# Attention's loads in another order: values and their shifted copy ahead of later K and Q

## Chip, core and metric

One core of a Trainium2 chip runs the whole program. Its engines are TensorE (PE, matrix products; PEld is its weight load), VectorE (DVE), ScalarE (ACT), GpSimd (POOL) and SyncE (SP). SP computes nothing here: it issues nearly all DMAs of the kernel, and 16 DMA engines carry them out. The metric is the device time of one execution in microseconds; lower is better.

## What is computed

The reference, cut to what matters. A windowed attention with 32 global tokens (4 batches, 8 heads, 512 local positions, head dimension 64) is followed by two feed-forward nets over 2176 tokens:

```python
def _attn_ref(q_l, k_l, v_l, q_g, k_g, v_g):
    k_all = np.concatenate([k_g, k_l], axis=2)
    v_all = np.concatenate([v_g, v_l], axis=2)
    out_g = np.matmul(sm(scale * np.matmul(q_g, k_all.transpose(0, 1, 3, 2))), v_all)
    s_ll = np.where(np.abs(pos[:, None] - pos[None, :]) <= 32, scale * q_l @ k_l^T, -1e9)
    s_lg = scale * np.matmul(q_l, k_g.transpose(0, 1, 3, 2))
    a_l = sm(np.concatenate([s_lg, s_ll], axis=-1))
    return np.concatenate([out_g, np.matmul(a_l, v_all)], axis=2)
...
x = attention output, 2176 x 512
h = x @ moe_w_in;   x = (h * cos(h)) @ moe_w_out
h = relu(x @ moe2_w_in);   result = (h * h) @ moe2_w_out
```

The weights come as 64-bit values, which the kernel reads as pairs of 32-bit words (`raw`) and converts.

## The kernel before, in words

The work on the attention is cut into 40 items (lines 667 to 677): for each group of four heads (8 groups, two for each batch) four local items, two for each pair of heads, and one global item. A pair of heads is p, a group is g = p // 2, so a group takes five items. One loop (line 1365) walks over steps s, some 3 us each. In a step every stage works on another item: `CFG['order']` (line 27) is the order of the stages inside a step, and `CFG['lag']` (line 29) says by how many steps a stage runs behind an item's scores. So TRK (transposing K on PE, tile tk) runs three steps ahead of the scores S (line 393), TRQ (transposing Q, tile tq) two steps ahead, SM (softmax) with them, TM (transposing the probabilities, tile tw) two steps behind, TE (ACT's copy of them to SBUF, tile tws) three, OM (the products with the values, tile o, or og for a global item) four. The order of the instructions of every engine is thus written out by hand; only what one engine needs of another is waited for.

Four of the stages are loads: LK, LQ and LV load K, Q and V of the group g + 2 (`load_k` line 252, `load_q` line 261, `load_v` line 267), and CV (`copy_v`, line 278) copies V inside SBUF, shifted by 64 rows: tile va to tile vb. All four are DMAs that SP issues, in the order of the program. A K takes five DMAs (one of 32 KB, one of 96 KB, three of 128 KB), a Q four of 128 KB, a V six, the copy two of 256 KB, the global values (`load_vg`, tile vgz, line 284) four of 32 KB, the global Q (`load_qgn`, line 384) and the tails of K (`load_ktn`, line 381) one of 64 KB each. K and Q have two buffers each, kn and qn, and V has two, va and vb.

K and Q of the groups 0 and 1, V of group 0 and its copy are issued ahead of the loop (lines 618 to 639). V of group 1 and its copy are issued inside the loop, by two lines at the end of a step (1423 to 1426).

SP issues one more kind of load in the loop: stage BG loads a first weight block (`conv_load`, line 110, tile raw, 512 KB) at step 5, a second at step 8, and four more. They are placed by a small planner, `piece` (line 1304): at step 5 + 3 * i at the earliest, with the conversion of a block three steps behind its load or later. That conversion is ACT's `conv_s` (line 147, tile cc) and POOL's `conv_u` (line 142, tile wf), also of stage BG, then DVE's `conv_v` and `conv_o` (lines 151 and 156) and POOL's `conv_c` (line 163). Inside a step ACT does TE, then BG, then KEV (copying K's transposes), then SM.

In the banks of PSUM tk, tq and tw take turns (`BT`, two banks), so a tw may start when ACT or DVE has copied out what stood in its bank two turns before; scores have three banks (`BS`).

Of the kernel before, what the change touches and what calls it, by code (L numbers as in the profile page):

```python
# [23 lines left out]
TWOPI = 2.0 * math.pi  # L24


CFG = {'order': ['CV', 'LQ', 'S', 'TE', 'BG', 'LK', 'OM', 'TRK', 'KEV', 'CC', 'SM',
           'RC', 'NM', 'CB', 'LV', 'OE', 'TRQ', 'QE', 'KC', 'TM'],
 'lag': {'S': 0,
         'TRK': -3,  # L30
         'TRQ': -2,
# [7 lines left out]
         'TE': 3,  # L39
         'OM': 4,  # L40
         'OE': 4,
         'LK': 0,
         'LQ': 1,
         'LV': 8,
         'CV': 11},
 'ndv': 1,
# [6 lines left out]
def kernel(  # L53
# [166 lines left out]
    BT, BG, BS, BO = (0, 1), (2,), (3, 4, 5), (6, 7)  # L220
# [20 lines left out]
    def whole(dst, src, c0, queues):  # L241

        n = dst.shape[2]
        if n == 2:
            for h, queue in enumerate(queues):
                queue.dma_start(dst[:, c0:4, h], src[h].rearrange("(c p) d -> p c d", p=P))
        else:
            for c in range(c0, 4):
                r = P * (c - c0)
                queues[0].dma_start(dst[:, c], src[:, r : r + P].rearrange("h p d -> p h d"))  # L250

    def load_k(gi, h=0, n=4, queues=(nc.sync, nc.sync)):
        b, g = gi // 2, slice(4 * (gi % 2) + h, 4 * (gi % 2) + h + n)
        if gi not in kn:
            kn[gi] = fp.tile([P, 4, 4, D], F32, tag="kn", name="kn", bufs=2)
        t = kn[gi][:, :, h : h + n]
        nc.sync.dma_start(t[0:SG, 0], k_g[b, g].rearrange("h p d -> p h d"))
        nc.sync.dma_start(t[SG:P, 0], k_l[b, g, 0 : P - SG].rearrange("h p d -> p h d"))
        whole(t, k_l[b, g, P - SG : SL - SG], 1, queues)

    def load_q(gi, h=0, n=4, queues=(nc.sync, nc.sync)):
        b, g = gi // 2, slice(4 * (gi % 2) + h, 4 * (gi % 2) + h + n)
        if gi not in qn:
            qn[gi] = fp.tile([P, 4, 4, D], F32, tag="qn", name="qn", bufs=2)
        whole(qn[gi][:, :, h : h + n], q_l[b, g], 0, queues)

    def load_v(gi):
        b, h0 = gi // 2, 4 * (gi % 2)
        va, g = VA[gi % 2], slice(h0, h0 + 4)
        nc.sync.dma_start(va[0:SG, 0], v_g[b, g].rearrange("h p d -> p h d"))  # L270
        for c in range(5):
            r0, r1 = (SG if c == 0 else 0), (SG if c == 4 else P)
            nc.sync.dma_start(
                va[r0:r1, c],
                v_l[b, g, P * c - SG + r0 : P * c - SG + r1].rearrange("h p d -> p h d"),
            )
# [14 lines left out]
    def tr_k(p):  # L291
        b, kk = divmod(p, NPAIR)
        tk = bank(BT, "tk")
        for c in range(4):
            nc.tensor.transpose(  # L295
                tk[:, c * P : (c + 1) * P],
                kn[p // 2][:, c, 2 * (p % 2) : 2 * (p % 2) + 2].rearrange("p h d -> p (h d)"),
                ident,
            )
        t = ep.tile([P, 8, KTB], F32, tag="kT", name="kT", bufs=3)  # L300
        kT[p] = t
        tks[p] = tk
# [3 lines left out]
    def k_evac(p):  # L306
# [4 lines left out]
        if p == 0:  # L311
# [6 lines left out]
            )  # L318
        if CFG["kb"] == "A":
            nc.scalar.activation(  # L320
                t[:, :, 128:KTB], tk[:, 0:SG].unsqueeze(1).to_broadcast([P, 8, SG]), AF.Copy
            )
        elif CFG["kb"] == "D":
            nc.vector.tensor_copy(
# [3 lines left out]
    def k_copy(p):  # L328
        if p == 0:
            return  # L330
        t = kT[p]
        one = dict(scalar1=1.0, scalar2=1.0, op0=ALU.mult, op1=ALU.mult)
        nc.gpsimd.tensor_scalar(t[:, 0:7, 64:128], t[:, 1:8, 0:64], **one)
        if CFG["kb"] == "P":
            nc.gpsimd.tensor_scalar(
                t[:, :, 128:KTB], t[:, 0, 0:SG].unsqueeze(1).to_broadcast([P, 8, SG]), **one
            )
        if p > 1:
            k_tail(p)
# [7 lines left out]
    def tr_q(p):  # L347
        tq = bank(BT, "tq")
        for c in range(4):
            nc.tensor.transpose(  # L350
                tq[:, c * P : (c + 1) * P],
                qn[p // 2][:, c, 2 * (p % 2) : 2 * (p % 2) + 2].rearrange("p h d -> p (h d)"),
                ident,
            )
        qT[p] = ep.tile([P, SL], F32, tag="qT", name="qT", bufs=3)
        return [lambda: nc.vector.tensor_copy(qT[p], tq)]
# [12 lines left out]
    def prep_ktail(b):  # L369
        nc.scalar.activation(ktail[:, :, b, 0:SG], tr_small(ktn, b, "ttail"), AF.Copy)  # L370
# [13 lines left out]
    def load_qgn(b):  # L384
        load_small(qgn, q_g[b], b)


    class Local:
# [57 lines left out]
        def norm(self):  # L446
# [7 lines left out]
            for u in range(4):  # L454
                (nc.vector if u < CFG["ndv"] else nc.gpsimd).tensor_scalar(
                    self.pt[:, u, 0:P],
# [14 lines left out]
        def t_evac(self):  # L471
            self.tws = lp.tile([P, 4, P], F32, tag="tws", name="tws", bufs=2)
            self.tgs = lp.tile([P, P], F32, tag="tgs", name="tgs", bufs=2)
            nc.scalar.activation(self.tws, self.tw, AF.Copy)
            if CFG["teg"][self.hb] == "D":
                nc.vector.tensor_copy(self.tgs, self.tg)
# [28 lines left out]
        def o_evac(self):  # L505
            c0 = self.b * SL + 256 * self.hb
            dst, src = xt[:, self.kk, c0 : c0 + 256], self.o.rearrange("p i q -> p (i q)")
            if CFG["oe"][self.hb] == "D":
                nc.vector.tensor_copy(dst, src)
# [127 lines left out]
    copy_v(0)  # L637
    load_k(1, 2, 2)
    load_q(1, 2, 2)
    nc.vector.memset(qgbd, 0.0)  # L640
    nc.gpsimd.memset(masks[0], 0.0)
    for h in range(2):
        s = slice(64 * h, 64 * h + 64)
# [16 lines left out]
    def spin(n):  # L660

        t = ps.tile([P, 512], F32, tag=f"bank{BO[1]}", name="spin")[:, 0:P]
        for _ in range(n):
            nc.tensor.matmul(t, lhsT=idle, rhs=idle, start=True, stop=True)
# [14 lines left out]
    def it(k):  # L679
        return items[k] if 0 <= k < NI else None  # L680
# [361 lines left out]
    S = [Step(s) for s in range(NS)]  # L1042
# [128 lines left out]
    order = [(s, i) for s in range(NS) for i in range(7)]  # L1171
# [193 lines left out]
    for s in range(L["TRK"], NI + L["OE"]):  # L1365
        due = lambda k: due_tr.get(s - k)
        qe = []
        for c in CFG["order"]:
            if c in ("BG", "CB", "CC"):
                for fn in bg[c].get(s, []):  # L1370
                    fn()
            elif c in ("TRK", "TRQ", "KEV", "KC", "QE"):
                p = due(L[c])
                if p is None:
                    continue
                if c == "TRK":
                    if p == 0:
                        spin(6)
                    tr_k(p)
                    if p == 0:  # L1380
                        spin(2)
                elif c == "TRQ":
                    qe = tr_q(p)
                    if p == 0:
                        spin(2)
                elif c == "KEV":
                    k_evac(p)
                elif c == "KC":
                    k_copy(p)
                elif c == "QE":  # L1390
                    for op in qe:
                        op()
            elif c in ("LK", "LQ", "LV", "CV"):
                p = due(L[c])
                if p is not None and p % 2 == 0 and p // 2 + 2 < 2 * B:
                    dict(LK=load_k, LQ=load_q, LV=load_v, CV=copy_v)[c](p // 2 + 2)
            else:
                i = it(s - L[c])
                if not i:
                    continue  # L1400
                if c == "S":
                    i.s_mm()
                    if s == 0:
                        prep_ktail(0)
                        k_tail(0)
                        k_tail(1)
                    elif s % 10 == 6 and s < 30:
                        prep_ktail(s // 10 + 1)
                    elif s % 10 == 3:
                        prep_qg(s // 10)  # L1410
                elif c == "SM":
                    for op in i.softmax():
                        op()
                elif c == "RC":
                    for op in i.recip():
                        op()
                else:
                    dict(NM=i.norm, TM=i.t_mm, TE=i.t_evac, OM=i.o_mm, OE=i.o_evac)[c]()
        if s in (8, 18):
            load_ktn(s // 10 + 2)  # L1420
        if s in (7, 17, 27):
            load_qgn(s // 10 + 1)
        if s == 2:
            load_v(1)
        if s == 5:
            copy_v(1)
        if due(0) is not None and due(0) // NPAIR + 1 < B:
            if due(0) % NPAIR == 2:
                load_vg(due(0) // NPAIR + 1)
        if s == XBOPEN:  # L1430
            first.close()
            open_pool("xb")
        if s == NI - 1:
            early.close()
            open_pool("s")
        if s >= NI - 1:
            emit(1.55 * (s - NI + 2))
# [39 lines left out]
```

## Time and profile before

| what | value |
|---|---|
| three runs, median (lowest to highest) | 874.62 us (874.11 to 876.35) |
| the profiled execution's own time | 874.08 us |
| its span, first to last instruction | 872.3 us |
| outside the span | 1.8 us |
| mean granted clock of TensorE | 0.997 |
| attention and its end | about the first 150 us |

The page gives the busy time of each engine and its share of the span. A timeline lists an engine's instructions in order of time: start and duration in us, engine, line, operation, tiles (written <- read), count, and in brackets the idle time before it with what ended it. SPq, PEq and so on are an engine's sequencer, which issues DMAs. A granted clock of 1.00 is the full 2.4 GHz, one of 0.50 is 1.2 GHz. Times are counted from the start of the span.

### The profile page before, as it was taken

Reading aid. Unit: us, or ns where it says so; the run is one execution under the profiler, and the core shown is the slowest. Engines: PE = TensorE matmul, PEld = TensorE weight load, DVE = VectorE, ACT = ScalarE, POOL = GpSimd, SP = SyncE. Lnnn points to the kernel's source line nnn. Section 1 sums busy time; section 2 is a strip of 40 time slices with the busy share of each in tenths; the row PEclk is TensorE's granted clock in tenths of the full one; section 3 lists DMA queues with packets and bytes.
Section 4 is the critical chain, followed back from the end, with each engine's and each line's share of the span. In section 5 each row is a group of like instructions: output and inputs, shape, how many; then the busy total and the mean of one; then the engine's idle time right before and its main releaser. Section 6 shows DMA issues by size and latency. Waiting matters only on the chain.

```text
span 872.3 us, 17134 instructions
## 1 busy us (share of the span) xinstructions
PE 849.8 (97%) x6028; PEld 782.7 (90%) x6028; DVE 655.6 (75%) x1409; ACT 530.7 (61%) x1275; POOL 582.1 (67%) x666
## 2 busy tenths in 40 slices
PE   7899999999999999999999999999999999999998
PEld 5677777899999999999999998889888989899886
DVE  6589997999798777967788798996755767454544
ACT  5689787887776656666555867655544554342331
POOL 6479898899887564758258899976645647432221
PEclk9999999999999999999999999999999999999999
DMA  7898665447875576557727546566864686446633
GB/s 159 192 222 191 138 215 173 186 179 248 298 275 183 201 302 260 177 173 301 272 79 260 216 171 266 190 228 238 279 209 139 238 302 218 134 166 249 215 118 85
DMA packets 134261, 182.00 MB, mean 209 GB/s; under 512 B 60960, under 2 KB 114720, under 8 KB 134176
## 3 DMA queue, kind: packets, MB, share of 16 engines
q1 hardware_dynamic: 130736, 179.79, 62.5%
q10 hardware_dynamic: 3440, 1.11, 0.5%
q8 instruction: 48, 0.79, 0.4%
q14 instruction: 37, 0.30, 0.1%
HBM read 141.03 MB, written 35.65 MB: 203 GB/s over the span
## 4 chain that ended last, share of the span: by engine, by line
PE 84%; DVE 6%; POOL 5%; ACT 2%; DMA 2%; issue 1%; SPq 1%; POOLq 0%; DVEq 0%; ACTq 0%
PE y L943 40%; PE hb L851 16%; PE ha L851 10%; PE he L851 10%; PE s L400 2%; DMA vb<-va 1%; PE o L484 1%; POOL xs L172 1%; PE o L496 1%; DVE pt L416 1%; POOL g L172 1%; PE og L602 1%; PE tk L295 1%; PE tw L468 1%; POOL wf L163 1%
## 5 line engine op out<-in xcount | busy, mean ns | idle before, releaser
L172 POOL TENSOR_TENSOR g<-cr,g 128x384 fp32r<-128x384 f32 (+1 forms) x192 | 203.1, 1071 | 146.0 <-ACT g L902 140.1
L954 DVE TENSOR_TENSOR xt<-y,xt 128x384 f32<-128x384 f32 (+2 forms) x287 | 170.2, 595 | 95.4 <-PE y L943 93.3
L943 PE MATMUL y<-g,wo 128*128 128x384 f32 (+1 forms) x1152 | 219.2, 327 | 0.4 <-DVE xt L954 0.4
L943 PE MATMUL y<-wo,g 128*128 128x512 f32 x816 | 209.4, 393 | 0.0
L943 PEld LDWEIGHTS y<-g,wo 128*128 128x128 f32 x1152 | 194.1, 188 | 1.5 <-ACT wo L205 0.7
L943 PEld LDWEIGHTS y<-wo,g 128*128 128x128 f32 x816 | 150.0, 188 | 24.1
L851 PE MATMUL hb<-xs,wi 128*128 128x384 f32 (+1 forms) x864 | 166.3, 327 | 1.3 <-ACT cr L891 1.2
L851 PEld LDWEIGHTS hb<-xs,wi 128*128 128x128 f32 x864 | 146.8, 188 | 7.5 <-ACT cr L891 1.6
L851 PE MATMUL he<-xs,wi 128*128 128x384 f32 (+1 forms) x576 | 111.0, 327 | 1.6 <-DVE he L865 0.8
L851 PE MATMUL ha<-xs,wi 128*128 128x384 f32 (+1 forms) x576 | 110.9, 327 | 1.2 <-DVE cr L894 0.7
L902 ACT ACTIVATE g<-cr 128x384 fp32r<-128x384 f32 (+1 forms) x192 | 93.7, 501 | 20.4 <-DVE cr L894 19.3
L163 POOL TENSOR_TENSOR wf<-wf,cc 128x512 uint32<-128x512 uint32 x64 | 87.7, 1376 | 26.4 <-DVE wf L151 18.2
L851 PEld LDWEIGHTS he<-xs,wi 128*128 128x128 f32 x576 | 98.0, 188 | 6.2 <-DVE cr L894 1.5
L851 PEld LDWEIGHTS ha<-xs,wi 128*128 128x128 f32 x576 | 97.6, 188 | 4.0 <-DVE cr L894 1.0
L156 DVE SCALAR_TENSOR_TENSOR cc<-raw,cc 128x512 uint32<-128x512 uint32 x64 | 63.0, 990 | 0.0
L888 ACT ACTIVATE cr<-cr,halfpi 128x384 f32<-128x384 f32 (+1 forms) x96 | 55.9, 592 | 11.2 <-DVE cr L883 9.9
L426 ACT ACTIVATE pt<-pt,st 128x160 f32<-128x160 f32 x128 | 53.1, 423 | 2.4 <-DVE st L416 2.3
L151 DVE TENSOR_SCALAR wf<-wf 128x512 uint32<-128x512 uint32 x64 | 49.6, 779 | 4.3 <-POOL wf L142 3.1
L859 ACT ACTIVATE s<-hb 128x384 f32<-128x384 f32 (+1 forms) x48 | 22.7, 473 | 48.8 <-PE hb L851 48.7
L147 ACT ACTIVATE cc<-raw 128x512 uint32<-128x512 uint32 x64 | 42.4, 669 | 15.1 <-DMA raw<-in_moe_w_in_dram 9.6
L859 ACT ACTIVATE s<-he 128x384 f32<-128x384 f32 (+1 forms) x48 | 22.6, 471 | 32.9 <-PE he L851 32.7
L416 DVE CUSTOM_DVE_ANT_0 pt<-s,mask 128x160 f32<-128x160 f32 x128 | 33.7, 318 | 11.5 <-PE s L400 11.0
(147 smaller groups left out, 1331.8 us busy)
## 6 DMA issues: line engine op xcount, KB each, us to landing
xs<-xs_T SPq DMA_DIRECT2D x48, 768.0 KB, 5.7
xs<-xs_B SPq DMA_DIRECT2D x36, 768.0 KB, 5.3
raw<-in_moe_w_in_dram SPq DMA_DIRECT2D x32, 512.0 KB, 5.1
raw<-in_moe_w_out_dram SPq DMA_DIRECT2D x32, 512.0 KB, 4.7
xs<-xs_T SPq DMA_DIRECT2D x24, 640.0 KB, 5.7
xs_T<-xs SPq DMA_DIRECT2D x16, 768.0 KB, 4.2
xs<-xs_B SPq DMA_DIRECT2D x18, 640.0 KB, 5.6
xs_B<-xs SPq DMA_DIRECT2D x12, 768.0 KB, 5.0
```

Of the source, the lines that this page charges most:

```text
L151: V.tensor_scalar(u, u, 3, None, op0=ALU.logical_shift_left)
L156: V.scalar_tensor_tensor(v, t[:, :, 1].bitcast(U32), 0x80000000, v, op0=ALU.bitwise_and, op1=ALU.bitwise_or,)
L163: G.tensor_tensor(u, u, v, op=ALU.add)
L172: eng.tensor_tensor(lo, x, hi.bitcast(F32), op=ALU.subtract)
L416: nc.vector.tensor_tensor_reduce(out=self.pt[:, u, :], in0=self.s[u // 2][:, 160 * (u % 2) : 160 * (u % 2) + 160], in1=m, scale=-0.125, sc ...
L426: nc.scalar.activation(self.pt[:, u, :], self.pt[:, u, :], AF.Exp, bias=self.st[:, 0, u : u + 1], scale=-1.0, accum_out=self.st[:, 1, u : ...
L851: nc.tensor.matmul(out, lhsT=w[:, ws, c : c + P], rhs=xs[:, xh, kk, 0:n], start=start and k == 0, stop=k == 5, skip_group_check=True,)
L859: A.activation(self.sb[name], self.hold(bank_name), AF.Copy)
L888: A.activation(self.r[key], self.r[key], AF.Sin, bias=halfpi, scale=TWOPI)
L902: A.activation(GT[s, f][0][:, th * n : th * n + n], self.r[key], AF.Copy)
L943: nc.tensor.matmul(o, lhsT=l, rhs=r, start=k == 0, stop=k == 5)
L954: V.tensor_tensor(dst, y, dst, op=ALU.add)
```

## The change

In the order of a step, LK comes from behind BG to the second place, LV from behind CB to behind OM, and LQ from the second place to behind LV; BG now stands behind all loads. LK is lagged by 2 instead of 0 and LQ by 3 instead of 1, so that K and Q are issued five steps ahead of their transposes and not seven. V of group 1 is issued ahead of the loop, and its copy at the end of step 2 instead of step 5. Nothing else is touched.

```diff
-CFG = {'order': ['CV', 'LQ', 'S', 'TE', 'BG', 'LK', 'OM', 'TRK', 'KEV', 'CC', 'SM',
-           'RC', 'NM', 'CB', 'LV', 'OE', 'TRQ', 'QE', 'KC', 'TM'],
+CFG = {'order': ['CV', 'LK', 'S', 'TE', 'OM', 'LV', 'LQ', 'BG', 'TRK', 'KEV', 'CC', 'SM',
+           'RC', 'NM', 'CB', 'OE', 'TRQ', 'QE', 'KC', 'TM'],
...
-         'LK': 0,
-         'LQ': 1,
+         'LK': 2,
+         'LQ': 3,
...
     load_k(1, 2, 2)
     load_q(1, 2, 2)
+    load_v(1)
...
         if s == 2:
-            load_v(1)
-        if s == 5:
             copy_v(1)
```

Written out, with a group's number in brackets, the order in which SP issues from the end of the lines ahead of the loop to the second weight block is:

```
before: K(2) Q(2) V(1) raw K(3) copy(1) vg(1) Q(3) qgn(1) | raw V(2)
after:  V(1) K(2) copy(1) Q(2) raw vg(1) K(3) qgn(1) V(2) Q(3) | raw
```

## Rows read from the trace of the kernel before

**Rows 1.** Page, part 1: busy us (share of the span) xinstructions.
```profile
PE 849.8 (97%) x6028; PEld 782.7 (90%) x6028; DVE 655.6 (75%) x1409; ACT 530.7 (61%) x1275; POOL 582.1 (67%) x666
```

**Rows 2.** Waits of PE, 0 to 180 us: us in total, times, longest us.
```profile
PE o L496 <- DMA vb<-va: 4.8, 2, 3.6
```

**Rows 3.** Timeline of PE, 14 to 52 us.
```profile
16.82 0.66 PE L350 MATMUL tq<-ident,qn 128*128 128x128 f32 x4 [1.19 <-ACT tws L474]
...
30.83 0.66 PE L295 MATMUL tk<-ident,kn 128*128 128x128 f32 x4
...
34.31 0.66 PE L350 MATMUL tq<-ident,qn 128*128 128x128 f32 x4
...
40.61 0.34 PE L496 MATMUL o<-tws,vb 128*64 128x64 f32 x4 [3.65 <-DMA vb<-va]
...
43.22 1.53 PE L400 MATMUL s<-kT,qT 64*64 64x160 f32 x16
...
51.72 0.60 PE L468 MATMUL tw<-ident,pt 128*128 128x128 f32 x4
```

**Rows 4.** Stretches: us, busy us of engines, granted clock, DMA share, GB/s.
```profile
0.00:36.00 36.00, 29.64 (x383) 23.28 (x385) 22.82 (x112) 23.18 (x87) 20.59 (x57) 1.00 0.82 177
36.00:41.00 5.00, 1.35 (x23) 1.07 (x21) 3.07 (x10) 1.59 (x8) 2.80 (x7) 1.00 0.78 164
41.00:45.10 4.10, 4.10 (x41) 3.26 (x38) 0.73 (x4) 2.85 (x8) 1.14 (x3) 0.58 0.89 232
45.10:60.00 14.90, 14.73 (x239) 12.01 (x235) 14.22 (x63) 11.70 (x47) 11.54 (x22) 1.00 1.01 212
```

**Rows 5.** Timeline of SP's DMA issues, 20 to 46 us.
```profile
20.71 0.44 SPq L257 DMA_DIRECT2D kn<-in_k_g_dram  x1
...
23.36 2.10 SPq L250 DMA_DIRECT2D qn<-in_q_l_dram  x4
...
27.64 2.37 SPq L273 DMA_DIRECT2D va<-in_v_l_dram  x2
...
30.05 0.52 SPq L117 DMA_DIRECT2D raw<-in_moe_w_in_dram  x1
...
33.27 1.00 SPq L280 DMA_DIRECT2D vb<-va  x1
...
41.47 0.44 SPq L117 DMA_DIRECT2D raw<-in_moe_w_in_dram  x1
42.02 0.44 SPq L270 DMA_DIRECT2D va<-in_v_g_dram  x1
42.50 3.13 SPq L273 DMA_DIRECT2D va<-in_v_l_dram  x5
```

**Rows 6.** Waits of SP, 36 to 41 us: us in total, times, longest us.
```profile
SPq L250 <- DMA vb<-va: 0.5, 1, 0.5
...
SPq L250 <- DMA kn<-in_k_l_dram: 0.4, 1, 0.4
```

**Rows 7.** DMA issues at 22.7, 27, 50, 33 us, KB each, us to landing; raw's landings.
```profile
kn<-in_k_l_dram SPq DMA_DIRECT2D x2, 128.0 KB, 2.9
...
va<-in_v_l_dram SPq DMA_DIRECT2D x3, 128.0 KB, 4.7
...
vb<-va SPq DMA_DIRECT2D x2, 256.0 KB, 4.0
...
vb<-va SPq DMA_DIRECT2D x2, 256.0 KB, 6.2
...
DMA to landing us min/median/max: 4.2/4.6/5.3
```

**Rows 8.** Timeline of ACT: the two weight conversions, and tws behind the first.
```profile
34.61 0.69 ACT L147 ACTIVATE cc<-raw 128x512 uint32<-128x512 uint32 x1 [0.21 <-DMA raw<-in_moe_w_in_dram]
...
36.85 0.58 ACT L474 ACTIVATE tws<-tw 128x512 f32<-128x512 f32 x1
...
47.72 0.71 ACT L147 ACTIVATE cc<-raw 128x512 uint32<-128x512 uint32 x1
```

**Rows 9.** Timeline of POOL: its half of the first weight conversion.
```profile
34.66 0.68 POOL L142 TENSOR_SCALAR wf<-raw 128x512 f32<-128x512 f32 x1 [0.55 <-PE tq L350]
```

## The prediction

> **What bounds the kernel now.** I began with the page: TensorE (PE) is busy 97% of an 872.3 us span [rows 1], so time comes back only where PE stands still or runs slowly. The waits of PE come next. In the first 180 us, attention and its end, PE waits 4.8 us for the shifted copy of the values (vb), in two waits, the longer of 3.6 us [rows 2]; no other load is named there for a wait after 14 us. PE's timeline has the place [rows 3]: before the first use of the second group's copy PE idles 3.65 us, to 40.61. The stretches by clock show a second price [rows 4]: from 41.0 to 45.1 us the granted clock averages 0.58, PE at its 1.2 GHz level after that idle time, at 2.4 GHz before and after. That costs 4.1 x 0.42 = 1.7 us. Elsewhere from 45.1 to 60 us PE is busy 14.73 of 14.90 us. So the **most that the change can give is 3.65 + 1.7 = 5.4 us**.
>
> Then SP's own timeline, since the change edits nothing else [rows 5]. SP issues back to back and lags: vb's copy, put at the end of step 5 (PE was past step 7's transposes, 30.83, by then), goes out at 33.27 us, behind K(2), Q(2), V(1), the first weight load (raw) and K(3) (numbers in brackets: the head group loaded). Its waits say why [rows 6]: a piece of Q(3) waits 0.5 us for the copy to land, though it reads nothing of it. Back through the code's order (three pieces of Q(3), four of VGZ, the copy's second half) that copy is the eighth DMA before it. So SP keeps at most eight in flight, and a slow landing holds every issue behind it; landings take 2.9 to 6.2 us [rows 7].
>
> **The change, part by part.** Engines other than SP keep their order, and POOL issues no DMA; what moves is when data land.
>
> *V(1) and its copy forward.* From 20.71 us, V(1)'s six DMAs now come first. K(2)'s five took 2.65 us there [rows 5], so six take 3.1; K(2) follows until 26.5. V(1)'s last piece is issued at 23.3 and lands 2.9 us later (K(2)'s piece in that place, [rows 7]), at 26.2, so the copy need not hold SP. Two issues at 26.5 to 27.6 land 4.0 to 6.2 us later [rows 7], at 30.5 to 33.8. Needed at 40.61 - 3.65 = 36.96: that wait is gone with 3 us to spare.
>
> *K(2) and Q(2) back.* K(2)'s last piece leaves at 26.0 and lands after 2.9 to 4.7 us [rows 7], at 28.9 to 30.7; its transposes stand at 30.83 [rows 3]: nothing, but if this cover of 0.1 us goes, PE waits up to 1 us. Q(2) leaves after the copies, to 29.9, or 31.2 if SP loses the 1.3 us it lost at 27.64, when two issues took 2.37 us instead of 1.05 [rows 5]. It lands by 32.2 to 35.3; transposes at 34.31: 0 to 1.0 us late, at no cost, since the next item is later still.
>
> *The first weight load is later.* Old order: 15 DMAs between 20.71 us and it; new: 17, the two copies being put ahead. It was issued at 30.05 [rows 5], and ScalarE (ACT) waited for it for 0.21 us, until 34.6 [rows 8]: **it has no slack**. Lower bound: the copies' two issues, 1.1 us. Upper bound: their 512 KB at the 232 GB/s of [rows 4] plus the 1.3 us stall, 3.5 us. I take 2.7, between them, nearer to the upper because both effects stand in the rows: from 34.6 to a landing at R = 37.3 (35.7 to 38.1). ACT runs in order: behind the conversion stand four exponentials and a tws, which ended 2.8 us after it began (34.61 to 37.43) [rows 8]; PE's next tw needs that bank, so R + 2.9 = 40.2. POOL's half of the conversion stands in the same step (34.66, 0.68 us) [rows 9], with VectorE's (DVE's) shift behind it, ahead of the normalising that the same tw needs and of the qT copy that the tk before it needs; the work behind each is no longer than ACT's 2.8 us. From there tw and tg 0.65, the score matmuls 0.70 and 0.65 for ACT's next ptg: PE ends that step's scores at R + 4.9 = 42.2, where before it ended at 43.22 + 1.53 = 44.75 [rows 3]. So of 5.4 us **2.55 are gained here** (4.1 to 1.7).
>
> *The second weight load is much later.* Old: 32 DMAs from 20.71 to its issue at 41.47. New: 38, since at step 8 V(2) and Q(3) now stand ahead of the background loads, where the weights stood ahead of V(2). V(2)'s six took 3.6 us [rows 5], so 45.1; less up to 0.9 that SP lost just there on the eighth DMA [rows 6], 44.2. I take 44.6. Landing 4.2 to 5.3 us, median 4.6 [rows 7]: R1 = 49.2 (48.4 to 50.4). ACT used to convert it at 47.72 and would now ask at 47.72 - 2.55 = 45.2: it stands 4 us, and with it four exponentials and the next tws that PE's tw waits for, the same work as behind the first, 2.8 us. That tw starts at R1 + 2.85 = 52.05, was 51.72 [rows 3]: **+0.3 us** (-0.5 to +1.5). The gain is given back whole.
>
> *The clock.* PE reaches that tw at 51.72 - 2.55 = 49.2 and idles 2.9 us. An idle of 1.19 us left the clock at 2.4 GHz, one of 3.65 us brought 1.2 GHz and cost 1.7 us [rows 3, 4]. 2.9 is nearer to 3.65: +1.7 (0 to 1.7).
>
> *The rest.* Third and fourth weight loads move ahead of K and Q and come earlier. Five steps last 51.72 - 30.83 less the 5.4 us lost, 15.5 us [rows 3]. That is what K(g+2) and Q(g+2) now have instead of seven steps. Q(g+2) queues on SP behind V(g+1), which waits for the og matmuls of the same step; V's 3.6 us, Q's 2.2 and a landing of 6.2 make 12.0: free, with 3 us to spare. V(2)'s copy, issued behind the second weight load, lands by 46.7 + 6.2 = 52.9 and is needed two steps after the tw at 51.72. With PE 99% busy to 60 us and no load named in its waits after, a shift passes through to the end.
>
> **Sum:** -5.4 (old wait and its clock) + 2.85 (first weight load) + 2.85 (second) + 1.7 (clock) = +2.0 us on this execution's 874.08, **876.1 us**. That execution is 0.5 us below the median of 874.62.
>
> **Rule against row.** For a load of 512 KB the rows show 4.2 to 5.3 us [rows 7]. The Trainium skill, DMA: Bandwidth & Descriptors, Anatomy of one DMA, gives (for DMAs issued by GpSimd) 2.0 us plus bytes over 436 GB/s; 3.2 us here, an estimate by that page. By it R1 would be 47.8, the tw 50.65, PE's idle 1.5, the clock kept: 873.0 us. The trace disagrees, and its rows stand.
>
> **Rivals.**
> *The weights come in time* (faster). If the second load lands by about 46.5 us, 2.55 us remain: 871.5; if the first does too by 34.6, 868.7. For it: DMA share is only 0.78 from 36 to 41 us [rows 4], so a better order has room. Against: 38 issues at 2.65 / 5 us are 20.1 us, to 40.9, and 4.2 more make 45.1 only if nothing holds SP at all; the old 32 took 20.8 us, 3.8 more than at that pace.
> *A quick second load* (no change). R1 at its lower bound of 48.4 gives the tw at 51.25, an idle of 2.05, nearer to 1.19, the clock kept: -0.5, 873.6. The page's 873.0 is the same case.
> *The second weight load stalls* (slower). If it is issued at 45.1 with the 1.3 us stall and lands in 5.3, R1 = 51.7, the tw at 54.55: +2.8, and the clock 1.7: 878.6. It decides from R1 = 49.8 on (0.9 + 1.7 = 2.6). For it: SP lost 1.3 us once already in the same stretch. Against: the median landing.
> *The copies come no earlier*, V(1)'s landing holding them beyond 37 us: as before, 874.1. Against: 3 us of margin.
>
> **How the numbers follow.** A measurement of this kernel tells 0.3% from no change, 2.6 us: 872.0 and 877.2. Forecast 0.35, quick second load 0.13, in time 0.20, stall 0.27, copies late 0.05. Faster 0.21 (in time, and a hundredth of the quick load); slower 0.29 (the stall, and the forecast's top); same 0.50. Cases of both signs hold half; the forecast's own range is 875.3 to 877.3 (R1 at its bounds, with the clock). The range of 8 in 10 runs from 871.0 (half of "in time") to 878.7.
>
> **What would show it.** Right: no PE wait on vb after 30 us; ACT's cc<-raw waits for the raw load at about 34.4 and 45 us, some 3 and 4 us; PE's tw waits for ACT near 49 us; a low clock shortly after. Wrong: ACT finds both weights landed and S of step 10 ends by 40 us (faster); or PE waits for Q(2) or K(2) near 31 to 37 us for over 2 us, which I price at nothing.

## The result and the profile after

The changed kernel takes **882.09 us**, the median of four runs (880.77 to 883.04). Four runs of the kernel before give 874.37 us (873.88 to 876.35). The ratio is 1.0085, with a 95% interval of 1.0068 to 1.0103: 7.7 us slower, where +2.0 was forecast and the range ended at 878.7. The sign was the forecast's, the size lies beyond even the stall rival's 878.6.

The profiled execution after took 882.11 us. Its page, part 1, against [rows 1]:

```profile
span 880.3 us, 17122 instructions
...
PE 858.6 (98%) x6028; PEld 789.5 (90%) x6028; DVE 651.9 (74%) x1409; ACT 530.7 (60%) x1275; POOL 582.7 (66%) x666
```

PE does the same 6028 instructions and is busy 8.8 us longer, while its idle time fell from 22.5 to 21.7 us (span less busy time). A loss that shows as busy time is one of slow work, or of stalls that took the place of others. The waits of PE, 0 to 180 us (us in total, times, longest us), show the stalls:

```profile
PE tw L468 <- ACT tws L591: 4.6, 1, 4.6
PE tk L295 <- DVE qT L356: 2.5, 2, 1.6
PE tk L295 <- DMA kn<-in_k_l_dram: 1.7, 3, 1.1
```

The wait for vb [rows 2] has left the list. In its place one wait of 4.6 us stands, for a copy that ACT made late. Who held ACT is in ACT's own waits, 0 to 180 us:

```profile
ACT cc L147 <- DMA raw<-in_moe_w_in_dram: 8.4, 2, 5.8
```

These are the two conversions of weight blocks. ACT's timeline has their places, against [rows 8]:

```profile
37.54 0.67 ACT L147 ACTIVATE cc<-raw 128x512 uint32<-128x512 uint32 x1 [2.63 <-DMA raw<-in_moe_w_in_dram]
...
52.33 0.66 ACT L147 ACTIVATE cc<-raw 128x512 uint32<-128x512 uint32 x1 [5.79 <-DMA raw<-in_moe_w_in_dram]
```

And PE's timeline has what they did to it, against [rows 3]:

```profile
37.30 0.29 PE L496 MATMUL o<-tws,vb 128*64 128x64 f32 x4
...
39.68 0.66 PE L295 MATMUL tk<-ident,kn 128*128 128x128 f32 x4 [1.63 <-DVE qT L356]
...
41.15 1.73 PE L400 MATMUL s<-kT,qT 64*64 64x160 f32 x16
...
55.17 1.12 PE L468 MATMUL tw<-ident,pt 128*128 128x128 f32 x4 [4.59 <-ACT tws L591]
```

The first use of vb stands at 37.30 without a wait, 3.3 us ahead of its old place at 40.61. PE ends step 10's scores at 41.15 + 1.73 = 42.88, 1.9 us ahead of 44.75; by 47 us it is 1.3 ahead. (From 23 to 37 us it had been 0.5 us behind: the last piece of K(1), issued ahead of anything that the change moves, landed 0.5 us later in this execution.) The tw that stood at 51.72 comes at 55.17, **3.45 us behind**. SP's timeline says why the second block lands so late, against [rows 5]:

```profile
26.80 0.47 SPq L280 DMA_DIRECT2D vb<-va  x1
...
28.37 2.73 SPq L250 DMA_DIRECT2D qn<-in_q_l_dram  x4
31.15 1.69 SPq L117 DMA_DIRECT2D raw<-in_moe_w_in_dram  x1
32.94 3.30 SPq L286 DMA_DIRECT2D vgz<-in_v_g_dram  x4
...
39.90 2.88 SPq L273 DMA_DIRECT2D va<-in_v_l_dram  x5
42.83 3.58 SPq L250 DMA_DIRECT2D qn<-in_q_l_dram  x4
46.46 0.51 SPq L117 DMA_DIRECT2D raw<-in_moe_w_in_dram  x1
```

The copies go out at 26.80, within the 26.5 to 27.6 of the prediction. The second raw goes out at 46.46, 5.0 us later than in the kernel before, behind V(2) and Q(3). Last, the stretches by clock (columns as in [rows 4]):

```profile
36.00:41.00 5.00, 3.31 (x42) 2.46 (x41) 2.61 (x9) 3.46 (x13) 2.24 (x5) 1.00 0.64 146
41.00:44.40 3.40, 3.40 (x40) 2.69 (x40) 2.84 (x14) 3.35 (x12) 3.00 (x7) 0.50 0.81 183
44.40:54.60 10.20, 6.18 (x106) 4.91 (x102) 4.72 (x24) 3.73 (x16) 5.18 (x8) 1.00 0.86 203
54.60:64.90 10.30, 9.73 (x82) 7.47 (x84) 5.76 (x22) 5.95 (x24) 5.85 (x12) 0.50 0.62 121
```

Between 20 and 65 us the clock has fallen to 1.2 GHz twice, not once as in [rows 4]. (One more stretch of 3.4 us, from 13.7 us on, which the kernel before does not have, ends ahead of the first DMA that the change moves, at 20.97.) After the idle of 1.63 us before 39.68 the clock is low for 3.4 us, as long as before the change; after the 4.59 us idle it is low for 10.3 us. In that stretch PE's 9.73 us of work would take half as long at 2.4 GHz, so it costs up to 4.9 us, an estimate from this row. From the tw at 55.17 on, PE's lag against the kernel before grows from 3.45 to 7.7 us while this stretch lasts, and then stays at 7.6 to 7.8 us until 153 us: 4.25 us were lost to the clock there, and 0.3 us more by the end (where 3.4 us at 1.2 GHz follow from 163.9 on) make the 8.0 us of the spans (880.3 against 872.3).

### The profile page after: what moved, and what is told of

It is laid out like the page before. It is cut to its first block, busy times and chain, and to the rows that moved or that the text cites. A ratio compares the mean times of both kernels' runs of the same rounds, so it can differ in the third digit from the quotient of the medians.

```text
span 880.3 us, 17122 instructions
## 1 busy us (share of the span) xinstructions
PE 858.6 (98%) x6028; PEld 789.5 (90%) x6028; DVE 651.9 (74%) x1409; ACT 530.7 (60%) x1275; POOL 582.7 (66%) x666
## 4 chain that ended last, share of the span: by engine, by line
PE 83%; DVE 6%; POOL 5%; ACT 2%; issue 2%; SPq 1%; DMA 1%; POOLq 0%; DVEq 0%; ACTq 0%
PE y L944 40%; PE hb L852 16%; PE he L852 10%; PE ha L852 10%; PE s L400 1%; POOL xs L172 1%; PE og L602 1%; DVE pt L416 1%; PE o L484 1%; ACT pt L426 1%; PE tw L468 1%; PE o L496 1%; POOL g L172 1%; DVE wf L151 1%; DMA raw<-in_moe_w_in_dram 1%
## 5 line engine op out<-in xcount | busy, mean ns | idle before, releaser
L151 DVE TENSOR_SCALAR wf<-wf 128x512 uint32<-128x512 uint32 x64 | 49.2, 773 | 5.2 <-POOL wf L142 5.2
L860 ACT ACTIVATE s<-hb 128x384 f32<-128x384 f32 (+1 forms) x48 | 22.7, 473 | 49.2 <-PE hb L852 49.1
```

The source lines that it names most:

```text
L151: V.tensor_scalar(u, u, 3, None, op0=ALU.logical_shift_left)
L860: A.activation(self.sb[name], self.hold(bank_name), AF.Copy)
```

## Experiments

Times are medians of 10 to 12 runs against the kernel before on the same chip (874.2 to 874.8); ratios carry a 95% interval. What is read from a timeline is one execution of each kernel. Three theories stood against each other. The first: the place of the second weight block in SP's order costs the time, through ACT and PE. The second: the values' copy or K and Q five steps ahead cost it. The third: the clock is a loss of its own beside the waits.

### 1. The changed kernel with the weights ahead of V and Q

```diff
-CFG = {'order': ['CV', 'LK', 'S', 'TE', 'OM', 'LV', 'LQ', 'BG', 'TRK', ...
+CFG = {'order': ['CV', 'LK', 'S', 'TE', 'BG', 'OM', 'LV', 'LQ', 'TRK', ...
```

> The changed kernel with one stage put back: in a step the weight blocks (BG) are again issued ahead of V and Q. Theory (the second weight load, held behind V(2) and Q(3), stops ScalarE, which stops PE and drops its clock): the load takes V(2)'s place in SP's queue, near 39.5 us, lands near 44 us, before ScalarE asks at some 46 us; its wait of 5.8 us and PE's wait of 4.6 us for tws go, and with them the low clock from 55 to 65 us. The first weight load is as late as in the changed kernel. 871 to 874 us. Rival (K and Q loaded five steps ahead instead of seven come late, or V ahead of them is what costs): still over 878 us, with PE waiting for kn or qn.

Measured 872.55 us, ratio 0.9987 (0.9976 to 0.9998): the whole loss is gone. SP's, ACT's and PE's timelines of this kernel, each a row:

```profile
39.19 0.45 SPq L117 DMA_DIRECT2D raw<-in_moe_w_in_dram  x1
```
```profile
37.66 0.67 ACT L147 ACTIVATE cc<-raw 128x512 uint32<-128x512 uint32 x1 [3.94 <-DMA raw<-in_moe_w_in_dram]
...
45.77 0.71 ACT L147 ACTIVATE cc<-raw 128x512 uint32<-128x512 uint32 x1
```
```profile
35.57 0.33 PE L350 MATMUL tq<-ident,qn 128*128 128x128 f32 x1 [1.40 <-DMA qn<-in_q_l_dram]
...
49.43 0.60 PE L468 MATMUL tw<-ident,pt 128*128 128x128 f32 x4
```

Issued at 39.19 and not 46.46, the second block is there when ACT asks, and the tw stands at 49.43 with no wait. The first block is as late as in the changed kernel, so the late first block is not what made that kernel slow. The early copy and the later K and Q are still in this kernel. They do cost something here: PE waits 1.40 us for Q(2), and the clock is at 1.2 GHz from 36.7 to 40.2 us. Yet the kernel is no slower than the kernel before, so the second theory, as the cause of the loss, falls too. The edit moves the later weight blocks forward as well, but the changed kernel's 7.7 us were lost by 65 us, ahead of ACT's conversion of the third block at 69.4.

### 2. The changed kernel with the conversions of these blocks later

The conversions of ACT and POOL come one step later for the first block and two for the second; the loads stay.

```diff
-        u = put("BG", {"G": 0.64}, ..., s + 3 + (i > 1), *needs)
-        c = put("BG", {"A": 0.66}, ..., max(s + 3 + (i > 1), summed.get(i - 2, 0) + 1))
+        u = put("BG", {"G": 0.64}, ..., s + 3 + (i > 1) + 2 * (i == 1) + (i == 0), *needs)
+        c = put("BG", {"A": 0.66}, ..., max(s + 3 + (i > 1) + 2 * (i == 1) + (i == 0), summed.get(i - 2, 0) + 1))
```

> The changed kernel, its loads in the same order, but the conversion of the first weight block one step later and that of the second two steps later, on ScalarE and GpSimd. Theory (only the place of the conversion in ScalarE's order makes the late loads cost): the loads land as before, at some 37.5 and 52 us, but the work that PE waits for is already past the first and mostly past the second; 869.5 to 874 us. Rival (the order of the loads costs by DMA traffic itself): over 878 us.

Measured 877.61 us, 1.0040 (1.0022 to 1.0057): a miss in the time. The stretch that the change spoiled behaves as expected. ACT's timeline:

```profile
53.20 0.67 ACT L147 ACTIVATE cc<-raw 128x512 uint32<-128x512 uint32 x1
```

The block landed at 51.25, 1.1 us earlier than in the changed kernel but still 5.2 later than in the kernel before, and held nobody; from 42 to 97 us PE was 0.7 to 2.1 us ahead of the kernel before. The time is lost further on. PE's waits from 90 to 160 us, and DVE's timeline:

```profile
PE ttail L362 <- DVE qT L356: 2.8, 1, 2.8
PE he L852 <- POOL xs L172: 2.1, 1, 2.1
```
```profile
96.50 0.94 DVE L151 TENSOR_SCALAR wf<-wf 128x512 uint32<-128x512 uint32 x1 [1.35 <-POOL wf L142]
```

In front of the first wait DVE stands 1.35 us for a weight block's conversion on POOL (wf), and the qT copy that PE needs comes behind it in DVE's order; from 98.8 us on the clock is then at 1.2 GHz for 3.4 us more. The second wait is for a piece of the planned background work on POOL (xs). Both waits are longer than any that the kernel before has between 90 and 160 us. That the later conversions push these pieces back fits the planner, which places each piece behind what it needs, but no run shows it apart. So a late block need not cost anything at the place where it lands, if nothing in order behind ACT's conversion is urgent; moving the conversion away cost more elsewhere: PE's lead of 2.1 us at 97 us has become a lag of 3.8 us at the end.

### 3. The kernel before with the values and their copy early, and nothing else

```diff
     load_q(1, 2, 2)
+    load_v(1)
...
         if s == 2:
-            load_v(1)
-        if s == 5:
             copy_v(1)
```

> The kernel before with one part of the change alone: V(1) issued ahead of the loop and its copy at the end of step 2; order and lags of before. Theory: the wait of 3.6 us for vb goes; the first weight load is still behind two more DMAs and late by 2 to 3 us, the second is the 33rd DMA as before and lands near 46 us, at most 1 us late; 871 to 874 us. Rival (V and its copy ahead of the weights are what costs): over 878 us.

Measured 873.70 us, 0.9997 (0.9986 to 1.0008). The vb waits fall to 1.4 us in total, but the first block lands at 38.4, 3.8 us later than in the kernel before, and PE waits 3.0 us for the qT copy behind it. One wait takes the place of another: the gain that the prediction looked for goes to the first weight block. The clock stays at 1.00 behind this 3.0 us wait, to 180 us. The second block, issued at 42.32, cost ACT 0.39 us.

### 4. The changed kernel with idle products in PE's 4.6 us wait

PE gets 18 products of a tile that nobody reads (36 instructions in the trace), ahead of the late tw.

```diff
+                    if c == "TM" and s == 12:
+                        spin(18)
                     dict(NM=i.norm, TM=i.t_mm, TE=i.t_evac, OM=i.o_mm, OE=i.o_evac)[c]()
```

> The changed kernel with 18 idle products of 128x128 on PE in step 12, just ahead of the transposes (tw) that wait 4.6 us for ScalarE. They add no result and fill most of that wait. Theory (the clock at 1.2 GHz from 54.6 to 64.9 us costs about 4.9 us of its own, beside the wait): PE runs at 2.4 GHz behind the wait and the kernel comes to 876 to 878.5 us. Rival (the clock costs nothing, as other engines bound that stretch): 881 to 883 us.

Measured 877.33 us, 1.0039 (1.0025 to 1.0054): 4.8 us less than the changed kernel had, or 4.0 by the two ratios, since the changed kernel was measured in another set of runs. ACT's timeline, PE's, and the stretch after it:

```profile
49.66 0.69 ACT L147 ACTIVATE cc<-raw 128x512 uint32<-128x512 uint32 x1 [4.71 <-DMA raw<-in_moe_w_in_dram]
```
```profile
48.50 4.18 PE L665 MATMUL spin<-idle 128*128 128x128 f32 x36
52.52 0.65 PE L468 MATMUL tw<-ident,pt 128*128 128x128 f32 x4
```
```profile
51.00:65.00 14.00, 13.61 (x200) 11.13 (x198) 10.83 (x46) 11.93 (x46) 9.95 (x21) 1.00 0.82 191
```

ACT still waits 4.71 us for the weights and the useful tw still comes late, but PE has work and the clock stays at 2.4 GHz. This profiled execution, 874.68 us, was the quickest of ten: the second block landed 2.7 us earlier in it than in the profiled execution of the changed kernel, and the clock stayed up behind the first block's stall too, where no idle product had run. So the medians carry the conclusion, and with them the mean granted clocks: 0.993 to 1.000 in the ten runs, 0.988 to 0.994 in the changed kernel's four. The clock is a loss of its own, near the 4.25 us read from the rows, and the rest is the late block; where the block landed in the other nine runs was not recorded, so the split is not exact.

### 5. The kernel before with V(1) in front and the copy where it was

```diff
     load_q(1, 2, 2)
+    load_v(1)
...
-        if s == 2:
-            load_v(1)
         if s == 5:
             copy_v(1)
```

> The kernel before with V(1) alone issued ahead of the loop; its copy stays at the end of step 5. The copy then has the same 20 DMAs ahead of it on SP as before. Theory (a load lands by its place in SP's queue, not by when its source is ready): vb comes as late as before, PE waits 3 to 4 us for it, 873.5 to 875.5 us, no change. Rival (V landing earlier lets the copy go earlier): the wait gone, 869 to 872 us.

Measured 874.79 us, 1.0009 (0.9997 to 1.0021), with PE's waits for vb at 4.5 us, the longest 3.9, as in [rows 2]. Loading the values early does nothing by itself; the copy's place is what counts.

### 6. The same, with the copy right behind the first weight block

The edit against the kernel of experiment 5:

```diff
                 for fn in bg[c].get(s, []):
                     fn()
+                if c == "BG" and s == 5:
+                    copy_v(1)
...
-        if s == 5:
-            copy_v(1)
```

> The kernel before with V(1) issued ahead of the loop and its copy right behind the first weight block in step 5, ahead of K(3); order and lags of before. SP's order is V(1) K(2) Q(2) raw copy(1) K(3), each load by the step that needs it. Theory: the first weight load has 15 DMAs ahead of it, as before, and lands at 34.6 to 36 us, the copy at 36 to 38 us, PE waits for each 1 us at most, the clock stays high, the second weight load is where it was: 868.7 to 871.5 us, the fastest of these kernels. Rival (the loads of this stretch cannot all come in time): 873 us or more.

Measured 874.98 us, 1.0010 (0.9995 to 1.0025): a miss, no gain. Issued at 30.04, the first block took 6.7 us to land beside the copy that followed it, ACT waited 1.80 us, and PE's vb waits still come to 3.4 us. The second block went out at 43.53, though no DMA had been added ahead of it, and four pieces of vgz took 3.95 us to issue, against 2.23 in the kernel before. ACT's and PE's timelines:

```profile
49.34 0.67 ACT L147 ACTIVATE cc<-raw 128x512 uint32<-128x512 uint32 x1 [3.73 <-DMA raw<-in_moe_w_in_dram]
```
```profile
52.17 0.66 PE L468 MATMUL tw<-ident,pt 128*128 128x128 f32 x4 [2.87 <-ACT tws L591]
```

Here PE idles 2.87 us and yet the granted clock stays at 1.00 from 46 to 180 us. The twelve runs spread from 872.8 to 878.2 us; those from 876 on have a mean granted clock of 0.990 to 0.996, those below 875 one of 0.994 to 1.000.

### 7. The kernel before with V(2) ahead of the second weight block

```diff
-CFG = {'order': ['CV', 'LQ', 'S', 'TE', 'BG', 'LK', 'OM', 'TRK', ..., 'CB', 'LV', 'OE', ...
+CFG = {'order': ['CV', 'LQ', 'S', 'TE', 'OM', 'LV', 'BG', 'LK', 'TRK', ..., 'CB', 'OE', ...
```

> The kernel before with one edit: V(2) is issued ahead of the weight block of the same step, so that the second weight load has six more DMAs ahead of it. Theory: it lands some 3 to 4 us later, near 49.7 us; ScalarE asks at 47.7 and waits 2 us; PE comes to its tw at 51.7 and waits about 1 us, at the high clock: 874.5 to 877 us. The changed kernel lost more because PE came to that place 1.3 us sooner and its clock fell. Rival (a late second weight load costs what it costs in the changed kernel): 880 us or more.

Measured 875.77 us, 1.0021 (1.0007 to 1.0034). The old vb wait stays (3.7 us), and the block goes out at 44.77, behind V(2). ACT's and PE's timelines:

```profile
50.53 0.69 ACT L147 ACTIVATE cc<-raw 128x512 uint32<-128x512 uint32 x1 [2.02 <-DMA raw<-in_moe_w_in_dram]
```
```profile
53.40 0.66 PE L468 MATMUL tw<-ident,pt 128*128 128x128 f32 x4 [0.84 <-ACT tws L591]
```

V(2) ahead of the weights makes a kernel slower that has nothing else of the change, if by little. PE's tw comes 1.7 us later than in the kernel before: 0.84 us of it is this wait, and most of the rest was there before the block was asked for, as the clock stayed at 1.2 GHz for 6.8 us behind the vb wait (39.0 to 45.8) and not for 3.4. PE runs later here than in the changed kernel, so the same kind of late block costs it only 0.84 us of idle time.

### 8. The kernel before with K and Q loaded five steps ahead, and nothing else

```diff
-         'LK': 0,
-         'LQ': 1,
+         'LK': 2,
+         'LQ': 3,
```

> The kernel before with the lags of the change alone: K and Q five steps ahead instead of seven; order of the stages, V(1) and its copy as before. SP's order becomes K(2) V(1) Q(2) raw copy(1) vg(1) K(3) qgn(1) Q(3) raw V(2): 15 DMAs ahead of the first weight load as before, the copy five places earlier than before, the second weight load in its old place. Theory (places of the weight loads and of the copy are all that counts here): PE's wait for vb 0 to 1.5 us, 869 to 872 us, faster than before. Rival (K and Q five steps ahead come late): PE waits for kn or qn by over 2 us, 874 us or more.

Measured 873.68 us, 1.0000 (0.9985 to 1.0016), against an expected gain: a miss by the median, though the waits came as expected (vb at most 1.0 us, ACT 1.20 and 1.98 us for the two blocks). Of the twelve runs seven lie from 872.0 to 873.8 us, at mean granted clocks of 0.998 to 1.000, and five from 875.6 to 877.4, at 0.990 to 0.996. K and Q five steps ahead are late for nobody (to 180 us PE's waits for kn come to 0.9 us, against 1.1 in the kernel before) and cost nothing by the median; they also take K(3)'s five issues from in front of the copy, which is why the vb wait shrinks. ACT's and PE's timelines:

```profile
46.38 0.70 ACT L147 ACTIVATE cc<-raw 128x512 uint32<-128x512 uint32 x1 [1.98 <-DMA raw<-in_moe_w_in_dram]
```
```profile
49.26 0.66 PE L468 MATMUL tw<-ident,pt 128*128 128x128 f32 x4 [1.16 <-ACT tws L591]
```

### 9. The same, with Q behind the weights

The edit against the kernel before:

```diff
-CFG = {'order': ['CV', 'LQ', 'S', 'TE', 'BG', 'LK', 'OM', 'TRK', ...
+CFG = {'order': ['CV', 'S', 'TE', 'BG', 'LQ', 'LK', 'OM', 'TRK', ...
...
-         'LK': 0,
-         'LQ': 1,
+         'LK': 2,
+         'LQ': 3,
```

> The kernel before with the lags of the change and the query load behind the weight block in a step, so that at step 8 the second weight load goes ahead of Q(3) and V(2). SP's order: K(2) V(1) Q(2) raw copy(1) vg(1) K(3) qgn(1) raw Q(3) V(2). Theory: the first weight load and the copy as in the kernel with the lags alone (1 us late each), the second weight load four places earlier, landed by 45 us, ahead of ScalarE, so that PE does not wait for its tws near 49 us: 870 to 873 us and, with the waits short, few executions in which the clock falls; faster than before. Rival (landings scatter from execution to execution by more than this margin): 873 to 875 us, no change.

Measured **872.13 us** (870.25 to 874.02), 0.9968 (0.9957 to 0.9979): faster than both kernels, 2.7 us below the kernel before. SP's, ACT's and PE's timelines:

```profile
39.56 0.45 SPq L117 DMA_DIRECT2D raw<-in_moe_w_in_dram  x1
```
```profile
44.91 0.72 ACT L147 ACTIVATE cc<-raw 128x512 uint32<-128x512 uint32 x1
```
```profile
48.59 0.60 PE L468 MATMUL tw<-ident,pt 128*128 128x128 f32 x4
```

The second block is issued at 39.56 and landed when ACT asks; the longest wait for vb is 1.1 us; the granted clock is 1.00 to 150 us. With the values where they were, a shorter queue ahead of the copy was enough.

## Why the prediction was wrong, step by step

**Right.** The copies' issue (26.8 in the range of 26.5 to 27.6), their landing by 33.5, and the end of the vb wait. K(2) and Q(2) cost nothing in this execution; for Q(2) that was luck. Its last piece landed at 35.06, when its transposes had begun at 34.82. In experiments 1 and 2, with the same order up to there, PE waited 1.40 and 1.60 us for it, and 3.4 us at 1.2 GHz followed each time; the prediction had priced it at 0 to 1.0 us "at no cost". The first block's landing, 37.5 for 37.3. The chain behind the second: ACT's conversion, four exponentials, tws, then PE's tw. Its length of 2.85 us, borrowed from the first block, is measured again in five kernels, wherever ACT waited for the block and PE for ACT, or PE spun meanwhile:

| kernel | conversion starts | PE's tw | difference |
|---|---|---|---|
| after | 52.33 | 55.17 | 2.84 |
| 4, idle products | 49.66 | 52.52 | 2.86 |
| 6, copy behind raw | 49.34 | 52.17 | 2.83 |
| 7, V(2) first | 50.53 | 53.40 | 2.87 |
| 8, lags alone | 46.38 | 49.26 | 2.88 |

Where the block is in time, as in 1 and 9, tw comes 3.7 us after the conversion and waits for nothing.

**The step that failed: "The second weight load is much later".** It had the mechanism and gave the landing R1 as 49.2, at most 50.4. It was 52.3. The issue was put at 44.6, at most 45.1, and came at 46.46; the landing was taken as the median of 4.6 us and took 5.9. The 38 issues from 20.97 took 25.5 us, 0.67 us each; I had priced them from the old order, as its 32 issues plus V(2)'s six, every issue at what it took there, less 0.5 us for the hold on the eighth DMA. That hold was gone indeed: in the kernel before Q(3)'s issues start at 38.51, 39.03, 39.60 and 40.49, each 0.02 to 0.06 us behind the landing of the eighth DMA before it, and in the changed kernel none of the 38 stands so close behind one. But Q(3)'s four took 3.58 us in their new place against 2.35 in the kernel before, and raw at 31.15 and the vgz behind it took 1.69 and 3.30 us against 0.52 and 2.23. That is 3.5 us more, where V(1)'s six took 1.35 us less (3.15 against 4.50). R1 came 3.1 us above the forecast; the tw came 3.45 us late where 0.3 was forecast, and this difference of 3.15 is R1's. It is the largest part of the 6.0 us between the forecast (+2.0) and the spans (+8.0). The stall rival had this direction and the landing at 51.7, with a chance of 0.27.

**The clock** is the second part: 1.7 us were forecast, for one stretch like the old one. Measured were a stretch of 3.4 us after the first block's stall, where the prediction had none (the scores there take 1.73 us, and the lead over the kernel before falls from 1.9 to 1.3; this only shortens the wait that follows, so it is no part of the total), and one of 10.3 us after the second, 4.25 us net by the rows and 4.0 to 4.8 by experiment 4. I had let the nearest idle time decide between 0 and 1.7. The runs show that the length of the idle time alone does not decide: one of 2.87 us left the clock at 2.4 GHz in experiment 6 and one of 3.03 us in experiment 3, while one of 2.78 us brought 3.4 us of 1.2 GHz in experiment 2 and one of 1.40 us the same in experiment 1; and in experiments 6 and 8 the time of one kernel varies along with its clock. A chance of each price was what the rows could carry, and a long one should have stood at the upper end.

**The sum again,** as it came: -1.3 at the first block (forecast -2.55, with the old wait's 5.4 inside; the 0.5 us from before the change's first DMA is in it), +4.75 to the tw (forecast +2.85), +4.25 clock (forecast +1.7), +0.3 later: +8.0 us of span.

**The estimate by the page** (the Trainium skill, DMA: Bandwidth & Descriptors, Anatomy of one DMA; 3.2 us for 512 KB, by a figure for DMAs issued by GpSimd) does not hold for these loads on SP's queue: both weight blocks after took 5.9 us or more, and the second blocks in experiments 1 to 9 took 4.5 to 5.8.

**What stays open.** Why the clock stayed low for 10.3 us here, against 3.4 us in the kernel before and in experiment 2 and 6.8 us in experiment 7 (39.0 to 45.8): the idle time before it was the longest, 4.59 us, but PE was then busy 9.73 of 10.30 us, and no run varied the idle time by itself. Why SP's issues sometimes take three times as long: in the changed kernel 2.0 us of SP's waits between 20 and 47 us are put down to PE and POOL, none over 0.7. Three single issues there took over 1.2 us: raw at 31.15 and, in SP's timeline:

```profile
33.49 1.79 SPq L286 DMA_DIRECT2D vgz<-in_v_g_dram  x1
```
```profile
43.92 1.94 SPq L250 DMA_DIRECT2D qn<-in_q_l_dram  x1
```

Beside each of these two, a packet of 16 KB goes over the queue that the profile lists as q8, instruction (from 33.46 us for 1.54 us and from 43.96 for 1.49); beside raw only one of 8 KB on q14 does. Over the eleven traces, from 20 to 66 us, 36 of 53 packets of 16 KB on q8 overlap an SP issue of 1.2 us or more, and 36 of the 47 such issues overlap one of them, though SP spends only 15% of that time in such issues. So SP's long issues and these packets go together; that the one causes the other was not tried. In the changed kernel the third of these packets after 20 us comes ahead of the second weight load's issue (43.96, the issue at 46.46), in the kernel before behind it (47.32, the issue at 41.47).

## What to carry to other kernels

When loads share one issuing queue, sort them by the time at which their reader asks, and count as reader the engine that runs in order: a transfer for later work is urgent if its conversion stands ahead of something that the critical engine needs. Before loads are moved forward, price the ones they are put ahead of at the mean pace of the whole queue, long issues and holds included (0.65 us an issue in the kernel before, 0.67 in the changed one), and leave the landing more room than a few landings show (4.2 to 5.3 us in the kernel before; 4.4 to 7.6 for the first two blocks over all kernels). The edit that only shortens the queue (K and Q later, Q behind the weights; 0.9968) gained at least as much as the one that also moves the values (0.9987).

## What was not expected of the hardware

- The granted clock stayed at its 1.2 GHz level for 10.3 us with PE busy 94% of that time, after an idle of 4.59 us. With idle products in that gap it stayed at 2.4 GHz in the profiled execution, and the median fell by 4.0 to 4.8 us, though they did nothing for the result.
- One kernel can take 872 or 877 us from one execution to the next, the longer times with the lower mean granted clock (experiment 8). A term for the clock is thus a chance, not a rule.
- One DMA of 512 KB from the same queue landed after 4.4 to 7.6 us (the first two weight blocks of each kernel; experiment 7's first, 29.03 to 33.47, and experiment 3's first, 30.75 to 38.40). The slowest had 512 KB of copies issued right ahead of it; of those with the copies right behind, experiments 6, 8 and 9 show 6.7, 5.6 and 7.4 us. So the copies beside it do not alone set its time.
